# Bulk loads of the first batch released in order, with weights moved into stage B of a Fourier-mixing and SwiGLU kernel

## Chip, cores and metric

One core of a Trainium2 chip runs the whole program. The metric is device time in microseconds.

## The reference

Eight batches of 3008 tokens with 256 features are filtered along the sequence in the frequency domain. Each token is then RMS-normalised and goes through a SwiGLU feed-forward layer of width 1536.

```python
X = np.fft.rfft(x, axis=1)                       # x: (8, 3008, 256)
y = np.fft.irfft(X * (filt_r + 1j*filt_i), n=3008, axis=1)
xn = y / np.sqrt(np.mean(y*y, -1, keepdims=True) + 1e-6) * rms_g
g = xn @ w_gate                                  # (24064, 1536)
out = (g / (1 + np.exp(-g)) * (xn @ w_val)) @ w_out
```

## The kernel before

The transform of length 3008 = 47 x 64 is done as matrix products. Batch 0 has nothing to overlap with, so its stages stand alone at the start. The names used below are these.

- **Stage A**: 12 products with `wa`, from x to `t1`; the result goes to a scratch `z` in HBM (`z_tmp`).
- **wi groups**: the inverse table `wi` is made on the chip from `wb`, in eight groups (TensorE transposes, ScalarE and VectorE evict). Its first block comes from HBM.
- **Stage B**: 16 units. Each multiplies a piece of z (tile `t2`, read back from `z_tmp`) with `wb`, multiplies by the filter (`fr`, `fi`), and multiplies with `wi` (product `psi`). In odd units one of the filter products is on GpSimd. The result goes to a scratch `g` in HBM.
- **t4 loads, first norms**: g is read back, the last inverse product is made, and the first tokens are normalised. After that the feed-forward products start (`pg`, `pv`), with everything of the later batches slotted in between.

These are the parts that the change touches. DMAs issued by `nc.gpsimd` cast from fp32 to fp16 where the tile is fp16 (x and the weights; the filters stay fp32).

```python
def a_unit(b, i):
    ...
    if b == 0 and i % 2:
        nc.vector.tensor_copy(out=dst, in_=src)
    else:
        nc.scalar.activation(out=dst, in_=src, func=AXT.Copy)

def f_load(c):                      # six to eight DMAs a chunk, 376 KB for fr, the same for fi
    for src, dst in ((filt_r, fr), (filt_i, fi)):
        nc.gpsimd.dma_start(...)
...
with tc.manual_schedule():
    for c in range(NXC):
        x_load(0, c)
    nc.sync.dma_start(wa, wa_d)
    nc.sync.dma_start(ident, id_d)
    for c in range(NC):             # NC = 4
        nc.vector.memset(fr[c][0:HALF], 0.0)
        nc.vector.memset(fi[c][0:HALF], 0.0)
        ...
        for i in range(3):
            a_unit(0, 3 * c + i)
        z_store(0, c)
    for c in range(NC):
        f_load(c)
    for q in range(4):              # w_gate, w_val, w_out, in quarters
        nc.gpsimd.dma_start(...)
    nc.sync.dma_start(wb, wb_d)
    for c in range(3):
        t2_load(0, c)
    nc.sync.dma_start(wi[:, 0], wi0_d)
    ...
    for g in range(8):
        wi_group(g)
    f_dup(0)                        # copies a filter chunk to the other 64 partitions
    for i in range(17):
        if i < 16:
            b_unit(0, i)
        if i % 4 == 1 and i // 4 + 1 < NC:
            f_dup(i // 4 + 1)
        if i >= 1:
            bi_unit(0, i - 1)
            if i % 2 == 0:
                g_store(0, i // 2 - 1)
        if i == 4:
            t2_load(0, 3)
    for c in range(NXC):
        t4_load(0, c)
    norm_first()
    ...
    rho_move(0, 1)
    for c in range(NXC):
        x_load(1, c)
    ...                             # cut: the feed-forward loop, unchanged
```

## Time and profile before

| | us |
|---|---|
| median time (3 runs) | 1030.96 |
| span of the profiled run | 1027.1 |
| first multiplication of stage B (VectorE) | 52.3 |
| last g store issued | 87.1 |
| first feed-forward product (`pg`) | 102.9 |

Two rows of the profile's picture in 40 slices, some 26 us each, show where to look. A digit is the busy share in tenths.

```profile
PE   2253989999999999999999999999999989999997
...
DMA  8952575324734356314834366315734333322111
```

TensorE is nearly full from the fifth slice on. In the first four it is not, and there the DMA engines are the busy ones in the first two. The table of stretches (start:end, length, then busy us and instruction count of PE, PEld, DVE, ACT and POOL, granted clock, DMA share, GB/s) says the same of the long rest:

```profile
103.00:1027.10 924.10, 898.77 (x6100) 549.22 (x6098) 552.63 (x919) 567.14 (x1005) 212.61 (x165) 0.99 0.42 101
802.20:920.90 118.70, 114.98 (x782) 70.57 (x781) 71.21 (x120) 73.23 (x130) 23.11 (x13) 0.99 0.35 94
```

So the change, which touches only the first 103 us, can gain there and nowhere else. The chain of waits (start, duration, what) of that part, with many links left out:

```profile
24.72 8.40 DMA z_tmp<-t_197
33.17 0.32 SPq L208
...
40.07 15.15 DMA wi<-wi_t
55.27 1.03 PE psi L235 x4
...
86.50 0.60 ACT t_563 L240
87.12 2.26 DMA g_tmp<-t_563
...
95.22 0.60 ACT sq L315
...
102.99 0.88 PE pg L362 x2
```

(The chain counts its piece of `pg` from 102.99; the instruction itself starts at 102.86, the 102.9 of the table.) The chain follows the DMAs. Some lines of the timeline (start, duration, engine, line, instruction; in brackets the idle time before it and what ended it) show that another path ran almost level with it:

```profile
25.18 0.46 SPq L458 DMA_DIRECT2D wb<-wb_t  x1
38.95 1.52 PEld L428 LDWEIGHTS <-wb 96*128 96x128 f16 x15 [25.17 <-DMA wb<-wb_t]
40.02 11.03 DVE L432 TENSOR_SCALAR wi<-pst 64x384 f16<-64x384 f32 x16 [16.64 <-ACT wi L430]
52.29 0.69 DVE L220 TENSOR_TENSOR s_327<-psb,fr_114 128x512 f16<-128x512 f32 x1
54.95 1.60 POOL L225 TENSOR_TENSOR s_335<-v,fi_118 128x512 f16<-128x512 f32 x1 [4.14 <-ACT v L224]
59.45 1.26 POOL L225 TENSOR_TENSOR s_367<-v,fi_118 128x512 f16<-128x512 f32 x1 [2.89 <-ACT v L224]
```

`wb` was issued at 25.2 us and landed at 38.9. The sixteen evictions of the wi groups followed on VectorE until 51. From the list of DMA issues, with count, KB each and median time to landing:

```profile
wb<-wb_t SPq DMA_DIRECT2D x1, 768.0 KB, 13.7
z_tmp<-t_197 SPq DMA_DIRECT2D x4, 96.0 KB, 8.4
t_250<-z_tmp SPq DMA_DIRECT2D x1, 384.0 KB, 13.3
g_tmp<-t_563 SPq DMA_DIRECT2D x1, 192.0 KB, 2.3
```

The first three travelled beside the filters and the weights; the last had the engines to itself.

### The profile page before, as it was taken

Reading aid. Unit: us, or ns where it says so; the run is one execution under the profiler, and the core shown is the slowest. Engines: PE = TensorE matmul, PEld = TensorE weight load, DVE = VectorE, ACT = ScalarE, POOL = GpSimd, SP = SyncE. Lnnn points to the kernel's source line nnn. Section 1 sums busy time; section 2 is a strip of 40 time slices with the busy share of each in tenths; the row PEclk is TensorE's granted clock in tenths of the full one; section 3 lists DMA queues with packets and bytes.
Section 4 is the critical chain, followed back from the end, with each engine's and each line's share of the span. In section 5 each row is a group of like instructions: output and inputs, shape, how many; then the busy total and the mean of one; then the engine's idle time right before and its main releaser. Section 6 shows DMA issues by size and latency. Waiting matters only on the chain.

```text
span 1027.1 us, 17356 instructions
## 1 busy us (share of the span) xinstructions
PE 934.9 (91%) x6279; PEld 569.6 (55%) x6279; DVE 604.7 (59%) x986; ACT 601.4 (59%) x1054; POOL 252.8 (25%) x225
## 2 busy tenths in 40 slices
PE   2253989999999999999999999999999989999997
PEld 0132556655665556655665566655665556656654
DVE  6462457644775467644775467644775457645553
ACT  1262755567656766567656766567656756556543
POOL 6431523031410323031411323031411312023200
PEclk9999999999999999999999999999999999999999
DMA  8952575324734356314834366315734333322111
GB/s 180 190 102 85 113 160 124 88 61 112 165 82 121 85 120 149 102 47 108 170 82 121 84 126 145 101 46 114 167 80 121 85 101 92 102 63 60 42 41 39
DMA packets 95349, 107.25 MB, mean 104 GB/s; under 512 B 17272, under 2 KB 70136, under 8 KB 94976
## 3 DMA queue, kind: packets, MB, share of 16 engines
q1 hardware_dynamic: 84768, 87.59, 32.6%
q0 software_dynamic: 10112, 17.77, 11.6%
q8 instruction: 49, 0.80, 0.3%
q10 hardware_dynamic: 384, 0.79, 0.2%
q14 instruction: 36, 0.29, 0.1%
HBM read 70.88 MB, written 49.90 MB: 118 GB/s over the span
## 4 chain that ended last, share of the span: by engine, by line
PE 75%; DMA 8%; DVE 5%; ACT 5%; issue 3%; SPq 2%; POOL 1%; ACTq 0%; DVEq 0%; POOLq 0%
PE pg L362 21%; PE pv L362 20%; PE psi L235 5%; PE psb L215 3%; SPq L204 2%; PE psn L267 2%; DMA wi<-wi_t 1%; PE psa L191 1%; ACT sq L276 1%; ACT y L274 1%; PE psq L284 1%; DMA z_tmp<-t_197 1%; DVE hh L367 1%; SPq L208 1%; DMA t_10462<-z_tmp 0%
## 5 line engine op out<-in xcount | busy, mean ns | idle before, releaser
L367 DVE TENSOR_TENSOR hh<-pv,sg 128x512 f16<-128x512 f32 (+1 forms) x576 | 391.0, 679 | 351.8 <-ACT sg L366 225.6
L366 ACT ACTIVATE sg<-pg 128x512 f16<-128x512 f32 (+1 forms) x576 | 340.5, 591 | 309.5 <-PE pg L362 307.0
L362 PE MATMUL pg<-xn,wg 128*128 128x512 f16 (+1 forms) x1152 | 340.9, 378 | 0.0
L362 PE MATMUL pv<-xn,wv 128*128 128x512 f16 (+1 forms) x1152 | 339.9, 377 | 0.0
L379 PEld LDWEIGHTS <-hh 128*128 128x128 f16 (+1 forms) x2304 | 221.7, 98 | 111.4 <-issue 33.8
L342 POOL TENSOR_TENSOR xn<-y,rb 128x1024 f16<-128x1024 f32 (+1 forms) x47 | 129.8, 2761 | 307.7 <-DMA rb<-r_tmp 238.3
L362 PEld LDWEIGHTS <-wv 128*128 128x128 f16 x1152 | 113.0, 98 | 132.7 <-issue 2.9
L296 POOL TENSOR_TENSOR rho<-u,mhalf 128x4 f32<-128x4 f32 x48 | 48.7, 1015 | 365.1 <-DVE u L294 348.9
L362 PEld LDWEIGHTS <-wg 128*128 128x128 f16 x1152 | 105.6, 98 | 21.8
L235 PEld LDWEIGHTS <-wi 128*128 128x128 f16 x512 | 51.8, 103 | 55.8 <-issue 12.2
L274 ACT ACTIVATE y<-psn,gsb 128x512 f32<-128x512 f32 (+1 forms) x94 | 64.3, 684 | 11.0 <-PE psn L267 6.0
L276 ACT ACTIVATE sq<-psn 128x512 f16<-128x512 f32 (+1 forms) x94 | 55.5, 590 | 0.0
L191 PE MATMUL psa<-xc,wa 128*128 128x512 f16 x96 | 37.5, 408 | 10.5 <-DMA xc<-in_x_dram 8.3
L215 PEld LDWEIGHTS <-wb 96*128 96x128 f16 x256 | 24.7, 104 | 35.9 <-issue 14.6
L175 POOL DMA_DIRECT2D xc<-in_x_dram x64 | 34.7, 559 | 0.8 <-POOLq L554 0.8
L428 PE MATMUL pst<-ident,wb 96*128 96x128 f16 x31 | 4.2, 310 | 27.2 <-DMA wb<-wb_t 24.3
L284 PEld LDWEIGHTS <-sq 128*128 128x128 f16 (+1 forms) x384 | 17.5, 97 | 14.4 <-ACT sq L276 2.1
L432 DVE TENSOR_SCALAR wi<-pst 64x512 f16<-64x512 f32 (+1 forms) x16 | 10.7, 671 | 16.9 <-ACT wi L430 16.6
L284 PE MATMUL psq<-ones,sq 128*128 128x1 f16 (+1 forms) x384 | 17.7, 165 | 3.1 <-ACT sq L276 1.8
L430 ACT ACTIVATE wi<-pst 128x512 f16<-128x512 f32 (+1 forms) x8 | 4.4, 584 | 27.4 <-PE pst L428 27.4
L191 PEld LDWEIGHTS <-wa 128*128 128x128 f16 x96 | 9.3, 100 | 18.7 <-issue 10.1
L428 PEld LDWEIGHTS <-wb 96*128 96x128 f16 x31 | 2.9, 138 | 29.1 <-DMA wb<-wb_t 25.2
(967 smaller groups left out, 1173.2 us busy)
## 6 DMA issues: line engine op xcount, KB each, us to landing
rb<-r_tmp SPq DMA_DIRECT2D x47, 256.0 KB, 4.1
xc<-in_x_dram POOLq DMA_DIRECT2D x56, 192.0 KB, 5.9
xc<-in_x_dram POOLq DMA_DIRECT2D x8, 160.0 KB, 6.7
wb<-wb_t SPq DMA_DIRECT2D x1, 768.0 KB, 13.7
wg<-in_moe_w_gate_dram POOLq DMA_DIRECT2D x4, 192.0 KB, 11.0
wv<-in_moe_w_val_dram POOLq DMA_DIRECT2D x4, 192.0 KB, 9.9
wo<-in_moe_w_out_dram POOLq DMA_DIRECT2D x4, 192.0 KB, 9.9
r_tmp<-rho SPq DMA_DIRECT2D x47, 2.0 KB, 2.1
```

The source lines that it names most:

```text
L191: nc.tensor.matmul(ps, wa, st[b]["x"][c][:, 2 * r:2 * r + 2, :], start=True, stop=True)
L215: nc.tensor.matmul(ps[:, u, :], wb[:, k, :], st[b]["t2"][k // KC][:, k % KC, :], start=True, stop=True)
L235: nc.tensor.matmul(ps[:, u, :], wi[:, 2 * i + u, q, :], s12[q][:, u, :], start=(q == 0), stop=(q == 1))
L274: nc.scalar.activation(out=y[:, dh, 0:w], in_=ps[:, 0:w], func=AXT.Identity, scale=gsb[:, dh:dh + 1])
L276: nc.scalar.activation(out=st[b]["sq"][m][:, dh, 0:w], in_=ps[:, 0:w], func=AXT.Square)
L284: nc.tensor.matmul(ps[0:w, q:q + 1], sq[:, dh, q * P:q * P + w], ones, start=(dh == 0), stop=(dh == 1))
L296: nc.gpsimd.tensor_tensor(out=rho, in0=u, in1=mhalf, op=ALU.pow)
L342: nc.gpsimd.tensor_tensor(out=xv[:, :, 0:nq], in0=yv[:, :, 0:nq], in1=rv[:, 0:nq].unsqueeze(1).to_broadcast([P, 2, nq, P]), op=ALU.mult)
L362: nc.tensor.matmul(ps[:, 0:w], wt[:, dt_, ts(jt, P)], xn[:, dt_, 0:w], start=(dt_ == 0), stop=(dt_ == 1))
L366: nc.scalar.activation(out=sg[:, 0:w], in_=pg[:, 0:w], func=AXT.Silu)
L367: nc.vector.tensor_tensor(out=hh[:, 0:w], in0=pv[:, 0:w], in1=sg[:, 0:w], op=ALU.mult)
L379: nc.tensor.matmul(po[s4 // 2][0:w, s4 % 2, :], hh[:, s4 * P:s4 * P + w], wo[:, jt, :], start=(jt == 0 and s4 % 2 == 0), stop=(jt == JT - ...
```

## The change

The intent is that transfers needed late should not be in the way of those needed soon. A tiny GpSimd copy (a "gate") reads one element of a tile. GpSimd issues the next bulk loads only when that element is there. Stage A's copies all go to ScalarE, so that none stands behind a memset on VectorE. `wb` comes in quarters, two of them at the very start. The weights come in halves inside stage B, and batch 1's x comes at stage B's last unit. A dummy Silu at the start loads ScalarE's table early.

```diff
-        if b == 0 and i % 2:
-            nc.vector.tensor_copy(out=dst, in_=src)
-        else:
-            nc.scalar.activation(out=dst, in_=src, func=AXT.Copy)
+        nc.scalar.activation(out=dst, in_=src, func=AXT.Copy)
 ...
+    def gate(ap):
+        g = up.tile([1, 1], FP32, tag="gate", name="gate")
+        nc.gpsimd.tensor_copy(out=g, in_=ap)
 ...                                  # cut: w_load(q) loads half q of the three weights, wb_load(c) a quarter of wb
     with tc.manual_schedule():
+        ...                          # cut: memsets of chunk 0, dummy Silu
         for c in range(NXC):
             x_load(0, c)
+        f_load(0)
         nc.sync.dma_start(wa, wa_d)
         nc.sync.dma_start(ident, id_d)
+        wb_load(0)
+        wb_load(1)
         for c in range(NC):
             ...
             z_store(0, c)
-        for c in range(NC):
-            f_load(c)
-        ...                          # cut: the weights in quarters
-        nc.sync.dma_start(wb, wb_d)
+        gate(st[0]["t1"][3][0:1, 5, 0:1])
+        f_load(1)
+        wb_load(2)
+        wb_load(3)
         for c in range(3):
             t2_load(0, c)
+        gate(st[0]["t2"][0][0:1, 0, 0:1])
+        f_load(2)
 ...
-        for g in range(8):
+        for g in range(4):
             wi_group(g)
         f_dup(0)
+        for g in range(4, 8):
+            wi_group(g)
         for i in range(17):
             if i < 16:
                 b_unit(0, i)
+            if i == 1:
+                f_load(3)
+            if i == 7:
+                w_load(0)
+            if i == 11:
+                w_load(1)
+            if i == 15:
+                for c in range(NXC):
+                    x_load(1, c)
 ...
         rho_move(0, 1)
-        for c in range(NXC):
-            x_load(1, c)
```

More of the change, by code (lines that the diff above doesn't have):

```diff
@@ L434, in wi_group, with w_load, wb_load @@
                                     scalar2=None, op0=ALU.mult)
-    with tc.manual_schedule():
+    def gate(ap):
+        g = up.tile([1, 1], FP32, tag="gate", name="gate")
+        nc.gpsimd.tensor_copy(out=g, in_=ap)
+    def w_load(q):
+        cols = ts(q, DFF // 2)
+        for src, dst in ((moe_w_gate, wg), (moe_w_val, wv)):
+            nc.gpsimd.dma_start(dst[:, :, cols], src.rearrange("(dt p) j -> p dt j", p=P)[:, :, cols])
+        nc.gpsimd.dma_start(wo[:, ts(q, JT // 2), :],
+                            moe_w_out.rearrange("(jt p) d -> p jt d", p=P)[:, ts(q, JT // 2), :])
+    def wb_load(c):
+        nc.sync.dma_start(wb[:, c * KC:(c + 1) * KC, :], wb_d[:, c * KC:(c + 1) * KC, :])
+    with tc.manual_schedule():
+        nc.vector.memset(mhalf, -0.5)
+        nc.vector.memset(fr[0][0:HALF], 0.0)
+        nc.vector.memset(fi[0][0:HALF], 0.0)
+        warm = up.tile([P, 4], FP32, tag="rho", name="warm")
+        nc.scalar.activation(out=warm, in_=mhalf, func=AXT.Silu)
         for c in range(NXC):
             x_load(0, c)
+        f_load(0)
         nc.sync.dma_start(wa, wa_d)
         nc.sync.dma_start(ident, id_d)
+        wb_load(0)
+        wb_load(1)
         for c in range(NC):
-            nc.vector.memset(fr[c][0:HALF], 0.0)
-            nc.vector.memset(fi[c][0:HALF], 0.0)
-            if c == 0:
-                nc.vector.memset(ones, 1.0)
-                nc.vector.memset(mhalf, -0.5)
+            if c:
+                nc.vector.memset(fr[c][0:HALF], 0.0)
+                nc.vector.memset(fi[c][0:HALF], 0.0)
             for i in range(3):
@@ L449 @@
             z_store(0, c)
-        for c in range(NC):
-            f_load(c)
-        for q in range(4):
-            cols = ts(q, DFF // 4)
-            nc.gpsimd.dma_start(wg[:, :, cols], moe_w_gate.rearrange("(dt p) j -> p dt j", p=P)[:, :, cols])
-            nc.gpsimd.dma_start(wv[:, :, cols], moe_w_val.rearrange("(dt p) j -> p dt j", p=P)[:, :, cols])
-            nc.gpsimd.dma_start(wo[:, ts(q, 3), :],
-                                moe_w_out.rearrange("(jt p) d -> p jt d", p=P)[:, ts(q, 3), :])
-        nc.sync.dma_start(wb, wb_d)
+        nc.vector.memset(ones, 1.0)
+        gate(st[0]["t1"][3][0:1, 5, 0:1])
+        f_load(1)
+        wb_load(2)
+        wb_load(3)
         for c in range(3):
             t2_load(0, c)
+        gate(st[0]["t2"][0][0:1, 0, 0:1])
+        f_load(2)
         nc.sync.dma_start(wi[:, 0], wi0_d)
```

## The prediction

> **What bounds it now.** After 103 us the kernel is bound by TensorE (table of stretches: PE busy 863 of the 887 us after 140 us, clock 0.99) and unchanged. The gain must come before it, where the slices show PE at 2 to 5 tenths and DMA at 8 to 10. The chain of waits there: VectorE copies between memsets (t_197 copied at 22.2 us, its x landed by 13.4), z store of t_197 issued 23.4, landed 33.2, z_tmp reads behind it, wi landing at 55.3 (15.2 us in flight), then stage B, 31 us at 4.2 us per two units (PE, DVE, ACT, POOL), to 86.5. wb, issued 25.2, landed 38.95; the eight wi groups take VectorE until 51. First wide matmul: 103.
>
> **Why the loads are slow.** From 2 to 58 us the DMA moves about 200 GB/s as landed; casting loads alone reach 170. A 384 KB z_tmp read takes 13.3 us there (t_250), 4.3 in quiet (t_393). The Trainium skill ("DMA: Bandwidth & Descriptors", "Issuing engines are not separate DMA queues") says all issuers interleave on the same 16 engines; the trace agrees. Filters (3 MB) and weights (2.4), mostly not yet needed, compete with z and z_tmp.
>
> **What the change does.**
> 1. Stage A: all 12 copies on ScalarE (0.60 us each), so none waits for a memset (1.76 us each, 17 us in all). The last ends near 17 us instead of 23.4. Half of wb beside x costs 1.5 us.
> 2. Four wi groups run at 18.5 to 24 us, after the memsets; the rest (1.42 us each) follow the other half of wb, near 27 to 33.
> 3. Estimate at 205 GB/s: x, half of wb, first filters and z (4.2 MB), plus part of the second filters: last z lands near 25.5 (was 33.2), first z_tmp read near 31 (46.5), wi near 36 (55.3). Stage B's first psi matmul: 36.5 instead of 55.3, 19 us gained (16 to 22).
> 4. Stage B keeps its pace: POOL idles 2.8 us of each 4.2, three weight issues (0.7 each) fit.
> 5. Given back: weights and batch 1's x (2.4 + 1.5 MB at 170 GB/s, 23 us) now start in mid stage B, so x is in flight during the last g store and the t4 loads. ScalarE issues half of those and waits for the first before its Square (8.1 us idle, to 95.2). Stores beside casting loads took 6 to 8 us instead of 2.3. Charged: 3.5 us (2 to 5).
> 6. Preloading the Silu table saves 1.28 us at 102.6, where PE does not wait: nothing.
>
> Net 19 - 3.5 = 15.5 us, all on the critical path: 1031 becomes **1015.5 us**, 80% range **1009 to 1021**. Chances: faster by over 2% (below about 1010) 0.17, within 2% 0.82, slower 0.01.
>
> **What would show it.** First psi matmul at 34 to 39 us; last z landed at 24 to 27; stage B 30 to 33 us long; last psi eviction to first Square 11 to 14 us (now 8.7); first wide matmul at 84 to 91; from there to the end unchanged within 2 us (924).
>
> **What would make it wrong.** If casting loads take less than half of the engines beside the stores, z and z_tmp land earlier and the gain passes 20. If batch 1's x starves the t4 loads, or POOL, blocked on DMA issues, holds up its multiplications in stage B, it falls to 10.

## The result, and the profile after

The changed kernel took 1017.69 us (median of 4 runs, 1016.69 to 1019.41) against 1031.01 us (4 runs, 1029.19 to 1031.17). The ratio is 0.9877, with a 95% interval of 0.9858 to 0.9895. A ratio is the mean time of one kernel's fast runs over that of the other's fast runs of the same rounds, so it is not quite the ratio of the medians.

The slices are too coarse to show a gain of a third of a slice on TensorE. They do show that the loads now run on into the third slice:

```profile
PE   2444989999999999999999999999999999999997
...
DMA  9994373325723474324824375314724343312211
```

The chain of waits, cut in the same way, has new members: two long stretches of DMA that the chain before did not have.

```profile
34.39 8.10 DMA fi_120<-in_filt_i_dram
42.49 0.28 issue
42.77 0.59 POOL fi_121 L410
43.38 1.28 POOL s_364 L222
...
70.86 0.60 ACT t_579 L237
71.48 9.66 DMA g_tmp<-t_579
...
86.71 0.60 ACT sq L312
...
94.56 0.88 PE pg L359 x2
```

The first: GpSimd stood in the six issues of a filter chunk, from 39.7 to 43.4 us, while unit 3's multiplication (`s_364`) waited behind them. The last of the six also waited 0.3 us for an earlier filter transfer to land and so free a semaphore (a credit, below); that is how the transfer comes into the chain. The second: the last g store took 9.66 us, where the same store had taken 2.26. Some lines of the timeline show the rest of what was different:

```profile
21.45 1.73 SPq L446 DMA_DIRECT2D wb<-wb_t  x2
28.54 1.62 PEld L425 LDWEIGHTS <-wb 96*128 96x128 f16 x16 [11.87 <-DMA wb<-wb_t]
29.81 5.62 DVE L429 TENSOR_SCALAR wi<-pst 64x512 f16<-64x512 f32 x8 [5.25 <-ACT wi L427]
35.47 0.69 DVE L217 TENSOR_TENSOR s_318<-psb,fr_114 128x512 f16<-128x512 f32 x1
38.13 1.60 POOL L222 TENSOR_TENSOR s_326<-v,fi_118 128x512 f16<-128x512 f32 x1 [2.10 <-ACT v L221]
43.38 1.27 POOL L222 TENSOR_TENSOR s_364<-v,fi_118 128x512 f16<-128x512 f32 x1
69.92 3.21 POOL L175 DMA_DIRECT2D xc<-in_x_dram  x6
```

Only eight evictions now stand between the later half of `wb` and the first multiplication. GpSimd's second multiplication follows 5.25 us after its first, where it had been 4.50. Batch 1's x starts at 69.9, just ahead of the last g store. The DMA issues, as before:

```profile
wb<-wb_t SPq DMA_DIRECT2D x4, 192.0 KB, 5.6
z_tmp<-t_208 SPq DMA_DIRECT2D x4, 96.0 KB, 7.8
t_233<-z_tmp SPq DMA_DIRECT2D x1, 384.0 KB, 3.8
g_tmp<-t_579 SPq DMA_DIRECT2D x1, 192.0 KB, 9.7
```

And the long rest, from the first feed-forward product on, with the same batch (the seventh) taken out:

```profile
94.50:1015.20 920.70, 896.56 (x6103) 549.21 (x6099) 552.35 (x919) 566.05 (x1004) 208.14 (x156) 1.00 0.41 99
793.50:909.00 115.50, 113.43 (x782) 70.08 (x782) 71.32 (x120) 73.10 (x130) 23.05 (x13) 1.00 0.37 96
```

Cutting both traces at the same events gives the account of the profiled pair, 1027.1 against 1015.2:

| stretch | before | after | gain |
|---|---|---|---|
| start to first multiplication of stage B | 52.29 | 35.47 | 16.8 |
| to the issue of the last g store | 34.83 | 36.01 | -1.2 |
| until that store has landed | 2.26 | 9.66 | -7.4 |
| to the first Square (`sq`) | 5.84 | 5.57 | 0.3 |
| to the first `pg` | 7.64 | 7.71 | -0.1 |
| **start to first `pg`** | 102.9 | 94.4 | **8.4** |
| first `pg` to the end | 924.3 | 920.8 | 3.5 |

The change thus won 16.8 us and gave half of it back before the first feed-forward product.

### The profile page after: what moved, and what is told of

Read it like the earlier page. It is cut to its first block, busy times and chain, and to the rows that moved or that the text cites. A ratio compares the mean times of both kernels' runs of the same rounds, so it can differ in the third digit from the quotient of the medians.

```text
span 1015.2 us, 17359 instructions
## 1 busy us (share of the span) xinstructions
PE 932.0 (92%) x6279; PEld 570.4 (56%) x6279; DVE 601.0 (59%) x980; ACT 602.4 (59%) x1060; POOL 249.1 (25%) x221
## 4 chain that ended last, share of the span: by engine, by line
PE 75%; DMA 8%; ACT 5%; issue 4%; DVE 3%; POOL 2%; SPq 1%; ACTq 0%; DVEq 0%; POOLq 0%
PE pg L359 21%; PE pv L359 20%; PE psi L232 5%; PE psb L212 3%; PE psn L264 2%; ACT sq L273 1%; SPq L201 1%; PE psa L191 1%; DMA g_tmp<-t_579 1%; DMA xc<-in_x_dram 1%; DVE hh L364 1%; PE psq L281 1%; DMA fi_120<-in_filt_i_dram 1%; ACT y L271 1%; PE po_12769 L376 0%
## 5 line engine op out<-in xcount | busy, mean ns | idle before, releaser
L232 PEld LDWEIGHTS <-wi 128*128 128x128 f16 x512 | 52.1, 103 | 54.2 <-issue 14.7
L271 ACT ACTIVATE y<-psn,gsb 128x512 f32<-128x512 f32 (+1 forms) x94 | 64.3, 684 | 10.4 <-PE psn L264 5.3
L212 PEld LDWEIGHTS <-wb 96*128 96x128 f16 x256 | 24.9, 105 | 36.0 <-issue 15.0
```

The lines of the kernel that those rows point to most:

```text
L212: nc.tensor.matmul(ps[:, u, :], wb[:, k, :], st[b]["t2"][k // KC][:, k % KC, :], start=True, stop=True)
L232: nc.tensor.matmul(ps[:, u, :], wi[:, 2 * i + u, q, :], s12[q][:, u, :], start=(q == 0), stop=(q == 1))
L271: nc.scalar.activation(out=y[:, dh, 0:w], in_=ps[:, 0:w], func=AXT.Identity, scale=gsb[:, dh:dh + 1])
```

## The experiments

Twelve kernels were run; all were correct. They share the changed kernel's code except where a diff says otherwise. "Changed kernel" below has the ratio 0.9877 to the kernel before, from the first session. Chips and sessions differ (the kernel before had medians of 1028.9 to 1031.5), so ratios are compared, and events in the traces, which are sharper. The intervals of the ratios are about 0.0025 to each side, or 2.5 us.

The theory after the result: stage B starts as soon as the deciding part of `wb` has landed and the wi groups behind it are done; the last g store suffers from batch 1's x; GpSimd's issue of filter loads costs the microsecond in stage B. The rivals: the weights' second half, still in flight until 72.9 us, holds up the store; the gates or the deferral do nothing; the z reads, not `wb`, start stage B.

### x of batch 1 put back (x_late)

```diff
-            if i == 15:
-                for c in range(NXC):
-                    x_load(1, c)
 ...
         rho_move(0, 1)
+        for c in range(NXC):
+            x_load(1, c)
```

> The changed kernel with batch 1's x loads put back behind the first norms, all else kept. Theory (x of batch 1 slows the last g store, which took 9.7 us instead of 2.3): the last g store lands within 2 to 5 us of its issue, the first wide matmul comes at 87 to 90 us instead of 94.4, the stretch after it stays 918 to 925 us, and the time is 1010 to 1013 us, 5 to 8 us below the changed kernel. Rival 1 (the second half of the weights, in flight until 72.9 us, is what the store waits for): the store still takes over 7 us and the time stays within 2 us of 1017.7. Rival 2 (the early x is what shortened the stretch after the first wide matmul from 924.3 to 920.8): that stretch grows by about 3.5 us and half of the gain goes.

It took 1010.16 us, a ratio of 0.9822 (0.9801 to 0.9842), which is 0.0055 or 5.7 us below the changed kernel's. The chain of waits of this run:

```profile
69.92 0.60 ACT t L237
70.54 2.29 DMA g_tmp<-t
```

The store landed in 2.29 us, although the weights were in flight until 70.7 us, that is, at the moment of its issue. The first `pg` came at 86.1 instead of 94.4. The rest took 922.0 us; since this stretch ranged from 920.8 to 924.7 over the profiled runs, no loss from the later x can be read in it. The growth that rival 2 expected (3.5 us) did not come; it was 1.2. The theory of the store is right as far as taking x away frees the store. Rival 1 is not ruled out by this run, since the weights were gone here, too, once the store was on its way; `w_early` below rules it out. The trace also shows that x is not the only load that slows a store: the g store issued at 62.2 us, beside the weights, took 7.1 us. Nothing waited for that one.

### The last filter chunk issued later (f3_late)

```diff
-            if i == 1:
+            if i == 3:
                 f_load(3)
```

> The changed kernel with the last filter chunk issued after the multiplication of unit 3 on GpSimd instead of unit 1. Theory (GpSimd stood in the issue of this chunk, waiting for a credit of an earlier filter transfer, while unit 3's operands were ready): unit 3's GpSimd multiplication starts 5.3 us after unit 1's in the changed kernel and 4.4 to 4.6 us after it here, stage B ends about 1 us earlier (last psi eviction near 69.8 instead of 70.86), time 1 us lower. Rival (stage B is paced by other things and the lost microsecond is the first unit's): no difference in stage B over 0.3 us.

The ratio was 0.9891 (0.9869 to 0.9913), no different from the changed kernel. GpSimd's multiplication of unit 3 did come 4.3 us after unit 1's instead of 5.25. But unit 5's then came 5.2 us after unit 3's instead of 4.0, because it now stood behind the same issues. The last g store was issued at 71.42 instead of 71.48. The mechanism was right and the remedy worthless: six issues of some 0.55 us each (3.3 us) do not fit between two multiplications, where GpSimd has some 2.7 us of each 4.0 to spare, wherever they are put.

### Without the gates (no_gates)

```diff
-        gate(st[0]["t1"][3][0:1, 5, 0:1])
 ...
-        gate(st[0]["t2"][0][0:1, 0, 0:1])
```

> The changed kernel without both GpSimd gates, so that the second and third filter chunks are issued as soon as GpSimd gets credits. Theory (the gates keep 1.5 MB out of the way of z and z_tmp): last z store lands 2 to 5 us later than 28.1 us, first z_tmp read 3 to 6 us later than 32.2, first multiplication of stage B at 38 to 42 instead of 35.5, time 2 to 5 us higher. Rival (the credits, one in eight transfers, already hold the filters back, so the gates do nothing): last z within 1 us, first multiplication within 1 us, and the issue block in stage B (unit 3's multiplication held up) vanishes, so the time is equal or 1 us lower.

The ratio was 0.9924 (0.9899 to 0.9948), some 4 to 5 us worse. The last z landed at 29.7 instead of 28.1, the third quarter of `wb` at 32.9 instead of 28.5, the first z read at 36.6 instead of 32.2, and the first multiplication came at 39.8 instead of 35.5. The gates are worth about 4.4 us of stage B's start. What else holds GpSimd back is a credit: in the traces of both kernels no DMA of GpSimd starts before the eighth before it has landed (the last filter issue, at 42.77 us, follows such a landing at 42.49). That alone does not hold the filters back far enough.

### Weights before stage B again (w_early)

```diff
         f_load(2)
+        w_load(0)
+        w_load(1)
 ...
-            if i == 7:
-                w_load(0)
-            if i == 11:
-                w_load(1)
```

> The changed kernel with both halves of the weights issued right behind the third filter chunk, before stage B. Theory (deferred weights are worth something only through GpSimd's queue and the z_tmp reads): the first z_tmp read is unchanged (32 us), later reads and wi land 2 to 5 us later, GpSimd stands in the weight issues so that its first multiplication comes at 43 to 50 us instead of 38.1; stage B ends 4 to 10 us later than 70.9; but with the weights gone by then the last g store has only x beside it and takes 6 to 9 us; time 1020 to 1027. Rival (the deferral of the weights brings nothing, only the order of the rest): time within 2 us of 1017.7.

The ratio was 0.9960 (0.9935 to 0.9985). Stage B's first multiplication on VectorE was unchanged at 35.4, but GpSimd, standing in the weight issues, came to its first at 43.8 and its second at 51.1; the last g store was issued at 79.1, 7.6 us late. That store again took 9.7 us, with the weights long landed (56.6) and only x beside it:

```profile
79.10 9.67 DMA g_tmp<-t
```

So the weights matter through GpSimd's queue, and x alone is enough to slow the store: this is the run that rules out rival 1. The delay expected for wi did not come (it landed at 36.7, in the changed kernel at 37.0).

### Wider runs in the g store (g_wide)

```diff
+    g0_d = nc.dram_tensor("g0_tmp", (KR, K2, D), FP16, kind="Internal").ap()
 ...                                  # batch 0 only; the t4 loads read it back in runs of 512 B
-        nc.sync.dma_start(g_d[b, 4 * c:4 * c + 4, :, :].rearrange("k p d -> p k d"),
-                          st[b]["t3"].pop(c))
+        dst = (g_d[b, 4 * c:4 * c + 4, :, :].rearrange("k p d -> p k d") if b else
+               g0_d[:, 4 * c:4 * c + 4, :])
+        nc.sync.dma_start(dst, st[b]["t3"].pop(c))
```

> The changed kernel, where batch 0's g scratch is laid out so that a g store writes runs of 2 KB (4 rows of 512 B) instead of 512 B, with x of batch 1 still beside the last store; the t4 loads then gather runs of 512 B instead of 3 KB. Theory (the DMA engines take turns by packet, so 384 packets of 512 B wait out as many packets of x, some 2.4 KB each): with 96 packets the last g store lands in 4 to 6 us instead of 9.7, x unchanged; the t4 loads get slower, since they now have small packets and meet the rest of x, so the first wide matmul may not come earlier. Rival (the two streams share by bytes, or the store's completion waits for something else behind x): the store still takes 9 us or more.

One look, 1015.23 us (a single run, state unknown). The DMA view of the time in which the last store was in flight (packets, MB, share of the 16 engines' time; q0 is GpSimd's queue with x, q1 SyncE's with the store), first of the changed kernel:

```profile
q0 software_dynamic: 645, 1.52, 87.4%
q1 hardware_dynamic: 498, 0.24, 9.5%
...
g_tmp<-t_579 SPq DMA_DIRECT2D x1, 192.0 KB, 9.7
```

and of this kernel:

```profile
q0 software_dynamic: 347, 0.87, 89.2%
q1 hardware_dynamic: 115, 0.20, 9.1%
...
g_tmp<-t SPq DMA_DIRECT2D x1, 192.0 KB, 5.9
```

The same bytes in fewer, larger packets landed in 5.9 us instead of 9.7, beside the same x. In both cases the store got under a tenth of the engines' time, and 0.24 of some 1.8 MB: the streams do not share by bytes. The Trainium skill ("DMA: Bandwidth & Descriptors", "Queues, rings and completion order") says that each engine goes round its queues packet by packet, a packet being several descriptors. This run agrees in direction: in the trace the data packets of x are of 3 KB (2.5 KB in the last pieces), those of the store of 512 B, here of 2 KB. It is not a clean proof of strict turns, and whether the profile's packets are those of the skill is not shown. A quarter of the packets took away half of the extra time (3.6 us over 2.3, instead of 7.4), not three quarters. The t4 loads paid as expected: from the landed store to the first Square 7.3 us instead of 5.6.

### Stage A's copies back on VectorE (dve_copies)

```diff
-        nc.scalar.activation(out=dst, in_=src, func=AXT.Copy)
+        if b == 0 and i % 2:
+            nc.vector.tensor_copy(out=dst, in_=src)
+        else:
+            nc.scalar.activation(out=dst, in_=src, func=AXT.Copy)
```

> The changed kernel with stage A's odd copies back on VectorE, between the memsets. Theory (the copies behind memsets delay the last z store, and the wi groups start later on VectorE): last z store issued at 21.5 to 24 us instead of 19.3, last z landed at 30 to 32.5 instead of 28.1, first multiplication of stage B at 37.5 to 39.5 instead of 35.5, time 2 to 4 us above the changed kernel's ratio of 0.9877. Rival (the last z store is paced by the stores before it, not by the copies): last z within 1 us, time within 1 us.

The ratio was 0.9968 (0.9938 to 0.9997), some 9 us worse, more than twice what was expected. The last z store was issued at 25.7, its landing came at 32.6, the third quarter of `wb` landed at 35.8 (7.3 us late) and the first multiplication came at 42.8 (7.3 us late). The direction was right, but the reach was mis-sized: `wb`'s later half is issued behind the z stores, so it is delayed with them. The profiled run of this kernel had a granted clock of 0.97 over the span; its events before 100 us are used here.

### wb in one piece again (wb_late)

```diff
-        wb_load(0)
-        wb_load(1)
 ...
-        wb_load(2)
-        wb_load(3)
+        nc.sync.dma_start(wb, wb_d)
```

> The changed kernel with wb loaded in one piece behind the z stores, as before. Theory (the early half lets four wi groups run under the loads, and the later half is what starts the last four): wb lands near 30 us, all eight groups follow in 11.4 us, first multiplication of stage B at 41 to 43 instead of 35.5; x lands 1 to 1.5 us earlier; time 5 to 7 us higher. Rival (stage B is limited by the z_tmp reads and wi, which land at 32 and 37, so the groups are mostly hidden): first multiplication at 36 to 38, time at most 2 us higher.

The ratio was 0.9964 (0.9934 to 0.9993), 9 us worse, where 5 to 7 were expected. `wb` landed at 30.0, all eight groups followed, and the first multiplication came at 43.35. The z read and the first block of wi had landed at 32.0 and 37.4, as in the changed kernel. They did not set the start.

### The deferral alone, on the kernel before (b_wdefer)

```diff
-        ...                          # cut: the weights in quarters, before wb
 ...
+            if i == 7:
+                w_load(0)
+            if i == 11:
+                w_load(1)
```

> The kernel before with one thing changed: the weights in two halves inside stage B. Theory (there the wi groups, released by wb at 38.9 us, hold VectorE until 51, so taking the weights away frees reads that VectorE is not ready for): first z_tmp read lands at 38 to 43 us instead of 46.5 and wi before 50 instead of 55.2, but the first multiplication stays at 50 to 52.5; time 0 to 2.5 us lower than before. Rival (the weights beside the z_tmp reads are the main cost of the kernel before): first multiplication at 44 or earlier, time 6 us or more lower.

The ratio was 1.0014 (0.9987 to 1.0042): no gain. The first multiplication came at 55.9 here, 3.6 us later than in the one profile of the kernel before, since `wb` landed at 42.5 instead of 38.9. Nothing that differs between the two kernels is issued before 32 us, and the last z store was already 0.7 us late at its issue, so part of this is how the saturated loads of one run differ from another's. The rest was not settled. The expectation also had the first z read at 38 to 43 us and wi before 50; they landed at 48.2 (46.5 before) and 52.1 (55.2 before). So this run does not test the theory that freed reads would have met a VectorE that is not ready: the first read was not freed. What is shown is only that the deferral, alone, brings no gain.

### All of wb early, x late (wb_all)

This and the last three runs look for a better version.

```diff
-        wb_load(0)
-        wb_load(1)
+        for c in range(NC):
+            wb_load(c)
+        nc.sync.dma_start(wi[:, 0], wi0_d)
 ...                                  # the later wb_load and wi0 go; x of batch 1 as in x_late
```

> The changed kernel with batch 1's x put back behind the first norms, and all four quarters of wb and wi's first block issued ahead of the z stores. Theory (in every run so far the first multiplication of stage B comes 6.97 us after the third quarter of wb lands, or 13.3 us after a wb in one piece: that load and the wi groups behind it start stage B): the third quarter lands before 12 us, all eight wi groups end on VectorE near 30 us, the first multiplication comes at 31 to 33.5 us instead of 35.5, now behind the first z_tmp read; x and z land 1 to 2 us later; first wide matmul at 82.5 to 85 us (86.1 with x late alone), time 1 to 3.5 us below x late alone, a ratio of 0.979 to 0.982. Rival (the z_tmp read and wi, not wb, set the start of stage B): wi groups end early but the first multiplication stays at 34.5 to 36 us, time unchanged from x late alone.

The ratio was 0.9829 (0.9805 to 0.9854), the same as x_late alone. The first multiplication came earlier, as the theory had it, at 33.35 (34.84 in x_late) and right behind the first z read. But nothing came of it. The timeline:

```profile
32.74 0.18 POOL L436 CAST gate<-t 1x1 f32<-1x1 f16 x1 [10.74 <-DMA t<-z_tmp]
...
35.44 1.75 POOL L410 DMA_DIRECT2D fi<-in_filt_i_dram  x2
37.30 1.29 POOL L222 TENSOR_TENSOR s<-v,fi 128x512 f16<-128x512 f32 x1
```

The gate opens when the first z read lands, and then GpSimd issues the third filter chunk until 37.2 us. Its first multiplication starts at 37.30, against 37.51 in x_late. Of the 1.5 us that VectorE gained, GpSimd could use 0.2. The first `pg` came at 85.9 (86.1 in x_late), where 82.5 to 85 were expected.

### The last chunk from SyncE's queue (wb_all_f3sp, f3_sp_i4)

```diff
-    def f_load(c):
+    def f_load(c, eng=nc.gpsimd):
 ...                                  # cut: its DMAs are issued by eng
-                f_load(3)
+                f_load(3, nc.sync)    # wb_all_f3sp: at unit 1; f3_sp_i4: at unit 4, behind the last z read
```

> The same, with the last filter chunk issued from SyncE's queue instead of GpSimd's. Theory (GpSimd, standing in the issue of this chunk, holds up a multiplication once, at unit 3 or wherever the chunk is put): with no such issue on GpSimd, the GpSimd multiplications of units 1, 3 and 5 are 4.3 and 4.0 us apart (5.3 and 4.0 in the changed kernel, 4.3 and 5.2 with the chunk after unit 3), and stage B ends about 1 us earlier than in the run beside it, unless the chunk on the SyncE queue delays the first g stores or z_tmp's last read. Rival (the lost microsecond comes from elsewhere): the spacing stays above 5 us at one place.

The ratio was 0.9873 (0.9851 to 0.9895), 4 to 5 us worse than wb_all. GpSimd's multiplications of units 1, 3 and 5 did stand 4.0 and 4.0 us apart. But SyncE, with nothing to hold it back, issued the last chunk at 31.2 us, ahead of the third at 32.9. The third chunk then held up VectorE's copy for 4.7 us and ScalarE's for 8.5 us, and unit 7's multiplication came 12 us after unit 5's. This is the cost that the gates are there to avoid, met by accident. (Granted clock 0.96 over this profiled run; the events are before 62 us.)

> The kernel of the run with all of wb early, with the last filter chunk on SyncE's queue, but issued only behind the last z_tmp read (unit 4), so that it can't overtake the third chunk. Theory (the issue on GpSimd costs stage B about 1.2 us; the chunk in the wrong order cost 8): GpSimd's multiplications of units 1, 3, 5, 7 stand 4.0, 4.0, 4.4 us apart, the third chunk lands by 43 us, no wait over 1 us for a filter, last g store issued near 69.5 instead of 70.7, first wide matmul near 84.7, time about 1 us below, a ratio of 0.981 to 0.983. Rival (SyncE's queue is simply slow for filters): the last chunk lands later than 55 us and holds up unit 9's copies, and stage B ends later than 71.

The ratio was 0.9802 (0.9779 to 0.9825). Units 1, 3, 5, 7 and 9 now stood 4.0, 4.0, 4.5 and 4.1 us apart, but the copy that needs the last chunk could start only at 56.6 us, and the next gap was 6.1 us. The last g store was issued at 71.3, no earlier than in wb_all (70.7). The theory was right, and what the rival foresaw came, too, and they cancel. But the rival's reason, a slow queue, is not borne out: the two 128 KB pieces of the chunk took 8.0 and 8.7 us from SyncE's queue, and 8.4 and 8.8 from GpSimd's in wb_all. The chunk was late because it was issued late, from 45.2 us instead of 38.5. The total is not told apart from x_late's 0.9822.

### The third chunk, too (filters_sp)

```diff
-        gate(st[0]["t2"][0][0:1, 0, 0:1])
-        f_load(2)
+        f_load(2, nc.sync)
```

> The same with the third chunk too on SyncE's queue, straight behind the z_tmp reads, and the second gate gone, so that GpSimd issues nothing while stage B starts. Theory (GpSimd, standing in the issue of the third chunk until 37.2 us, now sets the start of stage B): GpSimd's first multiplication at 35.7 to 36.3 us instead of 37.3, the next 4.0 to 4.5 us later; if the third chunk lands by 43 us, the last g store is issued at 67.5 to 69 and the first wide matmul comes at 82.5 to 84, a ratio of 0.979 to 0.982. Risk, and rival: the chunk takes over 8 us on this queue and lands after 44, holding up unit 5's copy, and stage B ends at 71 or later.

The ratio was 0.9804 (0.9772 to 0.9835). GpSimd's first multiplication came at 35.8, 1.5 us earlier than in wb_all; by unit 11 a gap of 6.4 us, again behind a late last chunk, had taken that back, and the last g store was issued at 70.1. The first `pg` came at 85.5 instead of 85.9. The four versions with late x other than wb_all_f3sp (0.9802 to 0.9829) cannot be told apart by their times. The simplest, x_late, beats both kernels of the study.

## Why the prediction was right, and where it was not

The time was right: 1015.5 was forecast with 1009 to 1021, and 1017.7 was measured. Taken point by point it was less good than that. At the first `pg` the gain was 8.4 us where 15.5 were forecast. Of the 7.1 us missing, 3.6 are what was given back (7.1 instead of 3.5), 2.2 are the start of stage B (16.8 instead of 19) and 1.2 its pace (forecast as unchanged). A gain after the first `pg`, where none was forecast, made up for most of it; that the total came out right is in this sense luck.

- **Stage B's start (points 1 to 3): right.** The first psi product was forecast for 36.5 and came at 37.0; the first z read was forecast near 31 and wi near 36, and they landed at 32.2 and 37.0. The last z landed at 28.1, later than the 24 to 27 given. By the prediction's own event, the first psi product, 18.2 us were gained of the 19; but GpSimd's first multiplication follows VectorE's by 2.66 us in both kernels, and it is GpSimd that stage B then waits for; by that event 16.8 count. What decided it was sharper than the prediction had it: not the z reads, but `wb`. In the seven runs with `wb` in two halves (changed kernel, x_late, f3_late, no_gates, w_early, g_wide, dve_copies) the first multiplication came 6.97 us after the third quarter of `wb` landed, at landings from 27.7 to 35.8. In the three with `wb` in one piece (before, wb_late, b_wdefer) it came 13.3 to 13.4 us after it. So of the 16.8 us gained there, 10.4 are the earlier landing (38.9 to 28.5) and 6.4 are the four groups taken out of the wait.
- **Stage B's pace (point 4): nearly right.** "Three weight issues fit" held: from unit 7 on the spacing is 4.0 to 4.5 us as before. What was overlooked is the filter chunk at unit 1, six issues and a wait for a credit: GpSimd's first step took 5.25 us instead of 4.50, 0.8 of the 1.2 us. Another 0.3 came at the step from unit 13 to 15 (4.35 instead of 4.03), where ScalarE started a copy late; why is not known. f3_late and wb_all_f3sp show the mechanism of the first. Counted from the first psi product to the last psi eviction, stage B took 33.8 us, outside the 30 to 33 given. The prediction had named this risk ("POOL, blocked on DMA issues") among what would make it wrong.
- **Given back (point 5): the mechanism was right, the size and place were off.** "Charged: 3.5 us (2 to 5)" was for store and t4 loads together; they cost 7.1 (7.4 lost, 0.3 regained). All of it fell on the one g store. The t4 loads, which I had charged, met almost no x any more, because the slow store kept them back until 81.3 us, and x had landed by 82.2. I took 6 to 8 us from z stores beside casting loads; these move 3 KB runs, and the g store moves 512 B (in runs of 2 KB, in g_wide, it took 5.9). x_late returns the whole term: 8.3 us at the first `pg` (7.4 are the store; the rest is a stage B that started 0.6 us earlier and ran 0.3 us shorter in that run), and 5.7 (by the ratios) to 7.5 us (by the medians) of the time.
- **"From there to the end unchanged within 2 us (924)": not so in the pair.** It was 920.8, a gain of 3.5 us. Nearly all of it is the seventh batch (118.75 against 115.43), where TensorE in the kernel before waited 2.8 us for a z read, and then ran products more slowly (granted clock 0.72 from 832 to 838 us; 1.00 in the changed kernel behind its wait of 1.2 us). The longer wait is 1.7 us of it, the longer busy time of PE over the batch (114.98 against 113.43) 1.6. Over all profiled runs this stretch ranged from 920.8 to 924.7. The changed kernel's is the shortest of all; the median of the eleven other runs with the new order is 922.2, so a part of the 3.5 us is the chance of this pair. The kernel before and b_wdefer, with the old order of issues, both had the 2.8 us wait in the seventh batch; in the twelve profiled runs with the new order it was 1.2 to 1.9 us. That is suggestive and not tested. Against it speaks that the same thing happens with the new order, too, in another batch: in the second batch of no_gates, w_early and filters_sp TensorE waited 2.1 to 2.6 us for a z read, the granted clock was 0.71 to 0.72 over the next 6 us, and the batch took 118.0 to 118.5 us (115.9 to 116.4 in the other new-order runs). What makes one of these waits long, and how much of the 13 us it makes up, stays open.
- **The first `pg`** was forecast for 84 to 91 and came at 94.4; "last psi eviction to first Square 11 to 14" came to 15.9. Those forecasts failed for the reason in point 5. The total was saved by the 3 to 5 us that came later and were not forecast (3.5 in the pair; 4.9 if the medians are taken).
- **The Silu table (point 6)**: not tested by itself. First Square to first `pg` is 7.6 before and 7.7 after, so no gain is seen there.

The parts do not add up. Taking one out costs 4 to 9 us each (gates, weights, wb, copies), and the whole gains 13. They lie on one chain, so each seems to protect what the others gain; and the deferral of the weights, alone, gained nothing.

## What to carry to other kernels

When a load is moved to a "free" place, look at what is in flight beside it there. Here the store on the chain, in runs of 512 B, took four times as long (9.7 us instead of 2.3), and moving the load past it (from 69.9 to 87.5 us) was worth more than any refinement of the rest. Before freeing DMA bandwidth, find the load, and the compute behind it, that decide; here `wb` and the wi groups behind it set the start, not the reads. Queue order is part of the schedule: an engine that issues bulk loads is not free to compute, and an ungated load on another queue can overtake the one that is needed first.

## What the Trainium skill lacked or had wrong

- "DMA: Bandwidth & Descriptors", "Queues, rings and completion order", has the round of queues by packet, but not what it costs: a 192 KB store in 512 B runs took 9.7 us beside a casting load, 5.9 us in 2 KB runs, 2.3 us in quiet.
- The same page, "Bandwidth", gives no rate for casting loads. With only such loads on the engines they moved 171 GB/s as landed (6 to 10 us of the kernel before, share of the engines over 100%), 0.68 MB in 4 us of fp32 to fp16. This counts the fp16 bytes that land; the fp32 bytes read are twice that, by estimate some 340 GB/s.
- The same page, "Anatomy of one DMA", puts dispatch at about 50 ns and calls descriptor generation "small, variable". It gives no time for which the issuing engine is held. On GpSimd's queue an issue here took 0.5 to 0.9 us (0.56 for x, 0.86 for half of `w_out`), and six in a row delayed its arithmetic by about a microsecond.
- "Issuing engines are not separate DMA queues" says several issuers save only issue time. The runs agree on bandwidth (8.0 and 8.7 us for two pieces of a filter chunk from SyncE's queue, 8.4 and 8.8 from GpSimd's), but the choice also decides order: the chunk moved to SyncE overtook the one on GpSimd and cost 4 to 5 us.
